# The last batch's channel products as seven block products, with sums of weight blocks kept in DRAM

## The chip, the core and the metric

The kernel runs on one core of one Trainium2 chip. A core has TensorE (matrix products into PSUM; PE in the profile, with PEld for the loading of the stationary operand), VectorE (DVE), ScalarE (ACT), GpSimd (POOL), and SyncE (SP), which here only issues DMA transfers. Each engine works through its own instructions in order and waits for the others on semaphores. The metric is the time of one execution on the device in microseconds.

## The reference

Four batches of 8 heads, 768 positions and 64 elements each go through an attention with a window of 16 positions to each side and 24 block summaries, and the result, x (768 x 512 per batch), through a mixer of two parts:

```python
xt = x.transpose(0, 2, 1)
h = np.maximum(xt @ w_tok1, 0.0) @ w_tok2       # tokens: 768 -> 256 -> 768
u = x + h.transpose(0, 2, 1)
h2 = np.maximum(u @ w_ch1, 0.0) @ w_ch2         # channels: 512 -> 1536 -> 512
return (u + h2).astype(np.float32)
```

The channel products are the largest part: per batch 768 x 512 x 1536, twice. Matrices come in float32 and results are close to float32: every operand of these products is kept as a high part in the TensorE's rounded float32 type and a low part (the rest), and a product is the sum of three: high by high, high by low, low by high.

## The kernel before

All of the program is written as pieces of work with an engine, an estimated duration, the data that they read and write, and a rank. `Plan` (L61 to L185) orders them: a list scheduler runs the engines in estimated time, each engine takes the ready piece with the lowest rank and then the lowest place in the program, and what comes out is the fixed order of every engine's instructions. The ranks are R_H, R_EVAC, R_ATT, R_LATER, R_W (0 to 4).

Buffers are `Slot`s under a tag with a number of buffers. The slots of one tag are taken in the order of the program: a slot's first piece waits until the slot so many places earlier is done with altogether (its stores to DRAM included), and comes no earlier than the first piece of the slot just before it (`_link`, L105 to L115).

Work is staged by batch. The main loop (L1142 to L1208) goes over the batches; for each, 24 slots: half 0 of the positions with 12 chunks of 128 hidden channels, then half 1 with 12. In batches 0 to 2 half 0 has 512 positions and half 1 has 256; in the last batch both have 384. In a slot, `ch1` (L829) makes one chunk of hidden channels, 12 matmuls into a bank with tag mm; ACT and DVE make its relu's high and low part, h. `ch2` (L866) adds that chunk's part to the four output banks acc0 to acc3, 12 matmuls. After the twelfth, `finish` (L917) adds u to the banks, on DVE its high part and on GpSimd its low part, and stores the result. For the half 1 of batches 0 to 2 its one output buffer has tag h.

Between these, the slots of batch b carry the attention of batch b + 1 (`att_step`), then `tok1x` (L703), which makes the first token product for two heads' pairs: three chunks, each with x and w_tok1 split on ACT and GpSimd into buffers xs and ws with tag u0, the products t1q on TensorE. `tok2` (L755) makes the second token product (up), adds x, and splits the sum into u's high and low part. For batches 2 and 3 x comes transposed by way of DRAM (`turn_x`, `fetch_x`). `tok2` for half 0 of batch b + 1 stands in slots 21 and 22 of batch b (23 in batch 0); for half 1 in slots 2 to 5 of batch b + 1 itself (0 for batch 0 and 1). Weights are loaded in batch 0 as 64-bit words, turned into float32 and split (`w_tick`, L997) into w1h, w1l, w2h, w2l, wt2h and wt2l, which stay in SBUF to the end. In the last batch four additions on GpSimd (`residual`, L904) prepare u for its second `finish`.

## Time and profile before

| | before |
|---|---|
| time of three runs | 581.9 us median (580.58 to 582.2) |
| span of the profiled execution | 579.3 us |
| its own time beside the span | the profile states none; the median is 2.6 us over the span |
| TensorE busy | 565.0 us, 98% of the span, 4701 matmuls |
| DVE, ACT, GpSimd busy | 288.2, 216.0, 154.1 us |
| granted TensorE clock | 0.994 of full speed |
| DMA | 75.89 MB, mean 131 GB/s |
| batch 0's first `hp` to batch 1's, 2's and 3's (start) | 65.9, 206.66, 339.53, 472.32 us |

The span is from the first to the last instruction of one execution. A matmul's busy time overlaps with its neighbours', as they are pipelined; how far apart the matmuls of one kind start is read from groups in the chain of waits, where a line has the start, the duration and the count. A group "a<-b" is an instruction that writes tile a and reads tile b. "idle before" is time in which an engine stood still just before such an instruction, with what ended it.

### The profile page before, as it was taken

The numbers are of one execution on the slowest core, as the hardware profiler recorded it, in microseconds if no ns is written. First come the engines' busy times: TensorE is split into PE (matmuls) and PEld (weight loads), VectorE is DVE, ScalarE is ACT, GpSimd is POOL, SyncE is SP. The second block draws the span as 40 slices with busy tenths as digits, with TensorE's granted clock in tenths as the row PEclk, the third lists the DMA queues.
The fourth block names the chain that finished last, engine by engine and source line by source line (L and its number), as shares of the span: only waits on it lengthen the run. The fifth ranks groups of instructions, "written<-read, shape, count | busy, mean of one in ns | idle before, by whom it ended". The sixth has DMA issues, their size and how long they took to land.

```text
span 579.3 us, 12315 instructions
## 1 busy us (share of the span) xinstructions
PE 565.0 (98%) x4701; PEld 500.2 (86%) x4701; DVE 288.2 (50%) x872; ACT 216.0 (37%) x697; POOL 154.1 (27%) x191
## 2 busy tenths in 40 slices
PE   7889999989999999999999999999999999999997
PEld 4678888768999988878899988888799999999997
DVE  3698799997563255644743336452543222112112
ACT  4777565436474343322333224222434111111110
POOL 0236586743033310000085010100085022005000
PEclk9999999989999999999999999999999999999999
DMA  8954568653565027846775127746454012001001
GB/s 281 325 159 129 182 200 262 220 164 129 188 190 161 18 76 197 230 121 188 204 192 131 23 55 189 195 139 139 117 146 81 1 34 59 1 1 54 1 1 54
DMA packets 116778, 75.89 MB, mean 131 GB/s; under 512 B 86640, under 2 KB 100080, under 8 KB 116720
## 3 DMA queue, kind: packets, MB, share of 16 engines
q1 hardware_dynamic: 116432, 74.72, 45.6%
q8 instruction: 37, 0.61, 0.4%
q10 hardware_dynamic: 288, 0.39, 0.2%
q14 instruction: 21, 0.17, 0.1%
HBM read 57.59 MB, written 15.73 MB: 127 GB/s over the span
## 4 chain that ended last, share of the span: by engine, by line
PE 82%; DVE 11%; DMA 3%; issue 2%; ACT 1%; SPq 0%; POOL 0%; DVEq 0%; ACTq 0%
PE acc L882 31%; PE hp L839 30%; PE t1q L736 5%; PE up L779 4%; PE av L559 4%; PE sc L428 4%; DMA w<-in_w_ch 2%; DVE wb L1067 2%; DVE wp L1060 1%; PE et L490 1%; PE warm L1108 1%; DVE wp L1053 1%; DVE wb L1060 1%; DVE vs L384 1%; DVE e L442 1%
## 5 line engine op out<-in xcount | busy, mean ns | idle before, releaser
L882 PE MATMUL acc<-h,w2h 128*128 128x512 f32 (+2 forms) x768 | 207.1, 340 | 2.2 <-DVE h L856 2.2
L839 PE MATMUL hp<-u,w1h 128*128 128x512 f32 (+2 forms) x768 | 192.7, 338 | 0.0
L882 PEld LDWEIGHTS acc<-h,w2h 128*128 128x128 f32 x768 | 135.8, 189 | 17.0 <-DVE h L856 3.4
L839 PEld LDWEIGHTS hp<-u,w1h 128*128 128x128 f32 x768 | 132.6, 189 | 12.3 <-issue 1.3
L856 DVE SCALAR_TENSOR_TENSOR h<-hp,h 128x512 fp32r<-128x512 f32 (+2 forms) x96 | 53.1, 553 | 153.8 <-ACT h L851 153.8
L839 PE MATMUL hp<-u,w1l 128*128 128x512 f32 (+2 forms) x384 | 129.1, 336 | 0.3 <-POOL w1l L1095 0.3
L882 PE MATMUL acc<-h,w2l 128*128 128x512 f32 (+2 forms) x384 | 129.1, 336 | 0.0
L851 ACT ACTIVATE h<-hp 128x512 fp32r<-128x512 f32 (+2 forms) x96 | 46.9, 488 | 201.4 <-PE hp L839 200.4
L452 ACT ACTIVATE e<-e,den 128x120 f32<-128x120 f32 x192 | 73.3, 385 | 48.6 <-DVE den L442 41.1
L839 PEld LDWEIGHTS hp<-u,w1l 128*128 128x128 f32 x384 | 72.5, 189 | 6.6 <-POOL w1l L1095 0.7
L882 PEld LDWEIGHTS acc<-h,w2l 128*128 128x128 f32 x384 | 72.6, 189 | 5.2
L943 POOL TENSOR_TENSOR ot<-ot,u 128x512 f32<-128x512 f32 (+2 forms) x28 | 27.9, 1021 | 116.8 <-DVE ot L935 116.8
L442 DVE CUSTOM_DVE_ANT_0 e<-sc,mask_sb 128x120 f32<-128x120 f32 x192 | 41.4, 277 | 13.7 <-PE sc L428 10.9
L779 PE MATMUL up<-wt2h,t 128*128 128x256 f32 (+2 forms) x128 | 37.6, 351 | 0.5 <-DVE xT L795 0.5
L411 POOL MEMSET e<- 128x48 f32 x16 | 2.2, 138 | 130.1 <-DMA away<-e 69.5
L452 ACT ACTIVATION_READ_ACCUMULATOR e<-e,den 128x1 f32 x192 | 36.3, 189 | 0.0
L722 POOL TENSOR_TENSOR xs<-x,xs 128x512 fp32r<-128x512 f32 x18 | 23.5, 1304 | 27.8 <-ACT xs L717 27.7
L428 PE MATMUL sc<-k,q 64*64 64x120 f32 x768 | 28.6, 275 | 1.9 <-PE et L490 0.7
L428 PEld LDWEIGHTS sc<-k,q 64*64 64x64 f32 x768 | 21.0, 134 | 10.5 <-issue 6.8
L736 PE MATMUL t1q<-xs,ws 128*128 128x256 f32 x216 | 28.9, 284 | 0.0
L559 PEld LDWEIGHTS av<-v,eT 120*64 120x64 f32 x768 | 24.0, 138 | 4.8 <-issue 2.3
L736 PEld LDWEIGHTS t1q<-xs,ws 128*128 128x128 f32 x216 | 27.3, 191 | 0.3
(73 smaller groups left out, 597.0 us busy)
## 6 DMA issues: line engine op xcount, KB each, us to landing
w<-in_w_ch SPq DMA_DIRECT2D x48, 256.0 KB
k<-in_kw SPq DMA_DIRECT2D x16, 720.0 KB
v<-in_vw SPq DMA_DIRECT2D x32, 288.0 KB
q<-in_q SPq DMA_DIRECT2D x16, 384.0 KB
away<-e SPq DMA_DIRECT2D x16, 384.0 KB
eT<-away SPq DMA_DIRECT2D x64, 96.0 KB
w<-in_w_tok SPq DMA_DIRECT2D x12, 256.0 KB
vb<-in_vb SPq DMA_DIRECT2D x32, 96.0 KB
```

The lines of the kernel that those rows point to most:

```text
L428: nc.tensor.matmul(tiles[j].t[c * QT : (c + 1) * QT, i * NC : (i + 1) * NC], lhsT=qt.t[rows, t * QT : (t + 1) * QT], rhs=kt.t[rows, t, :], ...
L442: nc.vector.tensor_tensor_reduce(out=e.t[:, j, i * P : i * P + NC], in0=tiles[j].t[:, i * NC : (i + 1) * NC], in1=mask_sb[:, mv, :], op0=A ...
L452: nc.scalar.activation(ei, ei, AF.Exp, bias=den_t[n].t[:, 1, T : T + 1], scale=-1.0, accum_out=den_t[n].t[:, 0, T : T + 1],)
L559: nc.tensor.matmul(pv[cs, T], lhsT=eT[:NC, T % (TT // 2), cs], rhs=v.t[:NC, 2 * T + c], start=True, stop=True,)
L722: lambda slot=slot, src=src: nc.gpsimd.tensor_tensor(out=slot.t[:, 1], in0=src(), in1=slot.t[:, 0].bitcast(F32), op=ALU.subtract),
L736: nc.tensor.matmul(pt.t[:, 2 * P * k : 2 * P * (k + 1)], lhsT=ws[:, wp, T, ks], rhs=xs[:, xp, T], start=(c == 0 and k == 0 and T == 0 and ...
L779: nc.tensor.matmul(pt.t[:, :nt], lhsT=t1.t[:, part, ks], rhs=w[:, k, h0 : h0 + nt], start=(far and k == 0 and i == 0), stop=(k == DTOK // ...
L839: nc.tensor.matmul(pt.t[:, :nt], lhsT=w[:, c, fs], rhs=us[c].t[:, part], start=(i == 0), stop=(i == len(ops) - 1),)
L851: lambda: nc.scalar.activation(h.t[:, 0], pt.t[:, :nt], AF.Relu),
L856: lambda: nc.vector.scalar_tensor_tensor(out=h.t[:, 1], in0=pt.t[:, :nt], scalar=0.0, in1=h.t[:, 0].bitcast(F32), op0=ALU.max, op1=ALU.sub ...
L882: nc.tensor.matmul(slot.t[:, c0 : c0 + nt], lhsT=w[:, f, o * P : (o + 1) * P], rhs=h.t[:, part], start=(f == 0 and w is w2h and part == 0 ...
L943: lambda view=view, u=u: nc.gpsimd.tensor_tensor(out=view(), in0=view(), in1=u.t[:, 1].bitcast(F32), op=ALU.add),
```

## The change

The two channel products of the last batch are written as 2 x 2 blocks and computed by Strassen's scheme (in Winograd's form) with seven block products in place of eight, in each of the two layers. For the first layer the blocks are: positions 0 to 383 and 384 to 767, input channels in two halves, hidden channels in two halves. For the second: the same positions, hidden channels in two halves, output channels in two halves.

- *Weight sums.* Four sums of weight blocks (s1 to s4) per layer and per pair of hidden chunks, 12 pieces in all. `weight_sums` makes a piece: five operations of 128 x 256 on GpSimd and five on DVE, then high and low part by two copies on ACT and two 128 x 512 subtractions on GpSimd, with a rank of its own, R_BACK, behind all others, and stores both parts to DRAM (2 x 512 KB). Four pieces stand in slots 13, 14, 15 and 17 of each of batches 0 to 2; those of slots 13 and 15 take two buffers each with tag u0, the others two with tag h. `weight_away` stores w2 as it is to DRAM too, in slots 0 to 11 of batch 1.
- *The last batch's input.* `tok2` of both its halves now stands in slots 20 to 22 of batch 2, with all of its x fetched in slots 18 and 19. The full sums stay in SBUF as u32, and of half 1 only the upper channels are split.
- *`last_mix`.* Takes the place of the last batch's 24 slots. It makes the four combinations of u (t1 to t4), on DVE (t1, t2) and GpSimd (t3, and t4's split), with t3's and one of t4's buffers under tag h. Then six steps k over pairs of hidden chunks, each with seven products of 6 matmuls, in the order 11, s2, (s4 and 22 of step k - 1), s3, 12, s1. They accumulate in three banks, which are read out by ACT and DVE between the products. GpSimd makes the combinations of the hidden blocks. The second layer has seven products of six steps, each step with a split on ACT and DVE and 2 x 3 matmuls. The sums s1 to s4 come from DRAM in rings (`first_load`, `second_loads`), in the second layer the single blocks too, into the space of w1 and other buffers. TensorE's order in `last_mix` is chained piece by piece.
- *Tiles.* Weights are per-chunk tiles (`w1_t`, `w2_t`) with high and low part side by side, in buffers that `last_mix` takes over. `residual` goes.

The diff, cut to its core:

```diff
-    w1h = const.tile([P, NC4, DFF], F32R, name="w1h")
...
+    w1_t = [sbuf([P, 2, NC4, P], "w1", f"w1_{f}", NF, F32R) for f in range(NF)]
+    w2_t = [sbuf([P, 2, DM], "w2", f"w2_{f}", NF, F32R) for f in range(NF)]
...
-    R_H, R_EVAC, R_ATT, R_LATER, R_W = range(5)
+    R_H, R_EVAC, R_ATT, R_LATER, R_W, R_BACK = range(6)
...
+    def weight_sums(w, k, tag):
+        blk, keys = blocks(w, k)
+        bufs = BUFS[tag]
+        z = sbuf([P, 4, 256], tag, f"sz_{w}_{k}", bufs)
+        hi = sbuf([P, 4, 256], tag, f"sh_{w}_{k}", bufs, F32R)
+        away = sd[w, k] = plan.slot(dram, [P, 2, 4, 256], F32, "sums", f"sums_{w}_{k}", 2 * HALF)
+        gate = state["gate"]
...
+        step("pool", 0, part("21", 0), part("22", 0), ALU.add)
+        step("pool", 0, own(0), part("21", 1), ALU.add)
+        step("pool", 0, own(0), part("22", 1), ALU.add)
+        step("dve", 2, part("11", 0), part("21", 0), ALU.subtract)
+        step("dve", 2, own(2), part("11", 1), ALU.add)
+        step("dve", 2, own(2), part("21", 1), ALU.subtract)
...
+        step("pool", 1, own(0), part("11", 0), ALU.subtract)
+        step("pool", 1, own(1), part("11", 1), ALU.subtract)
...
+        step("dve", 3, part("12", 0), own(1), ALU.subtract)
+        step("dve", 3, own(3), part("12", 1), ALU.add)
+        for ss in ((0, 1), (2, 3)):
...
+        add(
+            "sp", 0.06, lambda: nc.sync.dma_start(out=away.t[:, 0], in_=hi.t.bitcast(F32)),
...
+    def last_mix():
...
+        tmp = sbuf([P, 4, HS], "wt", "t32", 3)
+        tmp3 = sbuf([P, 2, HS], "h", "t33", 2)
...
+        for j in range(2):
+            both("dve", (tmp, j), (B12, j), (B11, j), ALU.subtract, R_ATT)
+            both("dve", (tmp, 2 + j), (B22, j), (tmp, j), ALU.subtract, R_ATT)
+            split((tmp, 2 + j), *ops["t2"][j], "dve", R_ATT)
+        for j in range(2):
+            both("pool", (tmp3, j), (B22, j), (B12, j), ALU.subtract, R_ATT)
+            split((tmp3, j), *ops["t3"][j], "pool", R_ATT)
...
+        def later(k):
...
+            first(k, "s4", b_, "22", False)
+            from_bank(c12, b_, c12, True)
+            first(k, "22", c_, "t4", False)
+            from_bank(c21, c_, c21, True)
...
+        for k in range(HALF):
...
+            first(k, "11", a_, "11", True)
...
+            first(k, "s2", b_, "t2", True)
+            from_bank(c21, b_, c12)
+            if k:
+                later(k - 1)
+            first(k, "s3", c_, "t3", True)
+            first(k, "12", a_, "21", False)
...
+            first(k, "s1", b_, "t1", False)
+            from_bank(c22, b_, c12)
+            from_bank(c22, c_, c22, True)
...
+        SECOND = (
+            ("11", "h11", "a"), ("s2", "t2", "b"), ("s3", "t3", "c"), ("s1", "t1", "b"),
+            ("12", "h21", "a"), ("s4", "h22", "b"), ("22", "t4", "c"),
+        )
...
-    for b in range(B):
+    for b in range(B - 1):
...
+            t2s = [(20, 0, 0), (20, 0, 1), (21, 1, 0), (21, 1, 1)]
+            t2s += [(22, 1, 2), (22, 1, 3), (22, 0, 2), (22, 0, 3)]
...
+            if b + 1 == B - 1 and slot in (18, 19):
+                for h in range(2):
+                    for p in (2 * slot - 36, 2 * slot - 35):
+                        fetch_x(b + 1, h, p)
...
+            for at_slot, tag in ((13, "u0"), (14, "h"), (15, "u0"), (17, "h")):
+                if slot == at_slot:
+                    n = len(sd)
+                    weight_sums(1 + n // HALF, n % HALF, tag)
+            if b == 1 and slot < NF:
+                weight_away(slot)
             ch2(b, half, f)
-            if last and 14 <= slot < 18:
-                residual(b, 1, slot - 14)
             if f == NF - 1:
                 finish(b, half)
+    last_mix()
     plan.write()
```

More of the change, by code (lines that the diff above doesn't have):

```diff
@@ L39 @@
 HS = S // 2
+HL = ((0, 0), (0, 1), (1, 0))
 HI_MAX = 122879.9921875
@@ L538, in fetch @@
             add(
-                "sp", 0.4, lambda r=r: part(r), reads=[(away, 0)], writes=[(slot, r)], kb=kb,
+                "sp", 0.4, lambda r=r: part(r), reads=[(away, 0)], writes=[(slot, key(r))], kb=kb,
             )
@@ L695, in tok1 @@
         add(
-            "pe", 2.8, products, reads=x_keys(b, p) + [("wt1", i) for i in range(3)],
+            "pe", 2.8, products, reads=x_keys(b, p) + [(wt1, i) for i in range(3)],
             writes=[(pt, 0)], rank=R_ATT,
@@ L790, in tok2 @@
         if far:
-            xT = xT_t.pop((b, half, p))
-            parts = [(xT, r) for r in range(P // 32)]
+            xT, parts = xT_t.pop((b, half, p))
             add(
@@ L845, in ch1 @@
             "pe", 12 * nt / 2220, products,
-            reads=[(u, i) for u in us for i in range(2)] + [("w1", f, 0), ("w1", f, 1)],
+            reads=[(u, i) for u in us for i in range(2)] + [(w1_t[f], 0), (w1_t[f], 1)],
             writes=[(pt, 0)], rank=R_W,
@@ new lines, in finish, with store @@
+            add(
+                "pool", spent(nt, 0.7, 1.2),
+                lambda view=view, u=u: nc.gpsimd.tensor_tensor(
+                    out=view(), in0=view(), in1=u.t[:, 1].bitcast(F32), op=ALU.add
+                ),
+                reads=[(u, 1)], writes=[key], rank=R_ATT,
+            )
+            store(b, h0, nt, o, view, [key])
+    def store(b, h0, nt, o, view, keys, queue="sp"):
+        eng = nc.sync if queue == "sp" else nc.scalar
+        add(
+            queue, 0.06,
+            lambda: eng.dma_start(out=out[b, o * P : (o + 1) * P, h0 : h0 + nt], in_=view()),
+            reads=keys, kb=nt // 2,
+        )
```

483 lines of the change are left out of this document (376 added, 107 removed).

## The prediction

> **What bounds the kernel now.** I read the page's busy shares, slices, transfers and chain of waits first, then TensorE's waits, then the last batch as one stretch. First the page.
>
> ```profile
> span 579.3 us, 12315 instructions
> PE 565.0 (98%) x4701; PEld 500.2 (86%) x4701; DVE 288.2 (50%) x872; ACT 216.0 (37%) x697; POOL 154.1 (27%) x191
> ...
> POOL 0236586743033310000085010100085022005000
> PEclk9999999989999999999999999999999999999999
> ...
> HBM read 57.59 MB, written 15.73 MB: 127 GB/s over the span
> ...
> PE 82%; DVE 11%; DMA 3%; issue 2%; ACT 1%; SPq 0%; POOL 0%; DVEq 0%; ACTq 0%
> ```
>
> TensorE is the bound: 98% busy at full clock, and the chain that ended last is its own work. So a matmul taken away is worth its spacing, as long as nothing that feeds TensorE becomes late. GpSimd is busy 27% on average, but in two bursts (the 85 and 085 of the slices), which matter below.
>
> TensorE's longest wait from 80 to 440 us (total, times, longest), the last batch as a stretch (busy time and count of PE, weight loads, DVE, ACT, GpSimd; clock; DMA share; GB/s), and how fast its matmuls follow each other (chain in order of time, columns start, duration, what):
>
> ```profile
> PE acc L882 <- DVE h L856: 2.2, 2, 1.8
> ```
> ```profile
> 472.30:575.40 103.10, 102.58 (x590) 101.80 (x588) 19.53 (x38) 13.69 (x28) 14.87 (x16) 1.00 0.09 21
> ```
> ```profile
> 478.48 2.08 PE acc L882 x12
> 480.56 0.02 issue
> 480.59 1.31 PE up L779 x6
> 481.89 2.08 PE hp L839 x12
> ```
>
> From the first matmul of the last batch (472.32, row below) to its last (575.24) there are 588 matmuls of 384 columns, 2.08/12 = 0.1736 us each. DVE, ACT and GpSimd are under 20% there, DMA at 9%: that is the cover for what the change adds. The `up` group took 1.31 where six spacings are 1.04: a group that TensorE has to wait for costs about 0.27 more on top of the wait.
>
> **The matmuls.** Before, the last batch's two layers are 2 x 288 = 576 matmuls. After, the first layer has 7 products x 6 steps x 6 matmuls = 252 and the second 7 x 6 x 2 x 3 = 252: 504, of the same shape, each with its own weight load as before. 504 x 0.1736 = 87.5 us. Of `up`, two groups of the last batch (588 - 576 = 12 matmuls, 2.1 us) move ahead of it. So 103.1 - 87.5 - 2.1 = **13.5 us** go; the 0.5 us of waiting and the slow `up` starts in the old stretch are in that.
>
> The tail stays: one DVE addition after the last matmul, one store of 192 KB, as in these rows. From 575.58 to the span's end are 3.7 us before and after.
>
> ```profile
> 575.24 0.34 PE L882 MATMUL acc<-h,w2h 128*128 128x384 f32 x1
> ```
>
> **The third product of the first step (s3 x t3).** t3 is made on GpSimd in a buffer with tag h. Buffers of a tag are taken in the order of the program, and that one comes behind the output buffer of batch 2's second half (`finish`), so the first of its instructions is put in order only when the first addition of that `finish` starts. From then GpSimd has, by rank and sequence, four `finish` additions ahead of most of t3. The rows are GpSimd's and DVE's timeline at that place, and the groups of its 384-wide work:
>
> ```profile
> 471.82 1.46 DVE L935 TENSOR_TENSOR ot<-acc,u 128x256 f32<-128x256 f32 x4 [1.28 <-PE acc L882]
> ```
> ```profile
> 472.32 2.81 POOL L943 TENSOR_TENSOR ot<-ot,u 128x256 f32<-128x256 f32 x4 [28.38 <-DVE ot L935]
> ```
> ```profile
> L856 DVE SCALAR_TENSOR_TENSOR h<-hp,h 128x384 fp32r<-128x384 f32 x24 | 13.3, 556 | 68.7 <-ACT h L851 68.7
> L851 ACT ACTIVATE h<-hp 128x384 fp32r<-128x384 f32 x24 | 11.8, 491 | 78.4 <-PE hp L839 78.4
> ...
> L808 POOL TENSOR_TENSOR u<-xT,u 128x384 fp32r<-128x384 f32 x4 | 4.1, 1015 | 9.7 <-ACT u L802 9.7
> ...
> L802 ACT ACTIVATE u<-xT 128x384 fp32r<-128x384 f32 x4 | 2.1, 524 | 9.8 <-DVE xT L795 9.8
> ```
> ```profile
> 472.32 0.52 PE L839 MATMUL hp<-u,w1h 128*128 128x384 f32 x2
> ```
>
> The additions start with the new batch (call it 0) and end at 2.81. Then the split of t3's first half (1.02, to 3.83), the subtraction for its second (to 4.84), ACT's copy (0.52 and two handovers of about 0.1, to 5.56), its split (to 6.58). TensorE has done 11 and s2 at 2.08; it takes the first four matmuls of s3 from 3.8 and the last two at 6.6, and ends s3 at 7.0 where 3 x 1.04 = 3.1 is due: **+3.9 us**. Queued behind it are 12, s1 and all later products (an order chained by hand). Ends: 0, if t3's instructions go ahead of the additions, and 6.8, if the weight sums of slot 17 still hold the output buffer (6.2 us of GpSimd by the prices below, half of it late). I take 3.9, the row's case. Three waits restart TensorE: 3 x 0.27 = **+0.8** (0 to 3).
>
> **The weight sums.** Twelve pieces, four in each of batches 0 to 2, at slots 13, 14, 15 and 17. Each has on GpSimd five 256-wide and two 512-wide operations, on DVE five 256-wide, on ACT two copies, on SP two stores of 512 KB. Prices:
>
> ```profile
> L1095 POOL TENSOR_TENSOR w2l<-wb,w2h x24: 737/748/1194, 58.5 to 133.3; 128x256 fp32r<-128x256 f32 x24
> ```
> ```profile
> L722 POOL TENSOR_TENSOR ws<-wt,ws x18: 1277/1290/1312, 163.4 to 442.6; 128x512 fp32r<-128x512 f32 x18
> ```
> ```profile
> 290.00:340.00 50.00, 50.00 (x427) 48.49 (x426) 18.77 (x37) 14.88 (x31) 21.09 (x20) 1.00 0.44 99
> 421.00:472.00 51.00, 51.00 (x439) 50.48 (x438) 15.35 (x32) 14.10 (x31) 20.23 (x16) 1.00 0.26 62
> ```
>
> GpSimd per piece: 5 x 0.75 + 2 x 1.29 = 6.3 us; four are 25 us. In the second halves of batches 1 and 2 it has 50 - 21.1 = 28.9 and 51 - 20.2 = 30.8 us free: they fit, barely. But slots 13 and 15 use tag u0, whose four buffers come ahead of those of `tok1x`: its first chunk now waits until slot 13's sums are in DRAM, its second until slot 15's are. In batch 1 the second half's `finish` additions are over at 294.7 (four of 1.28 from 289.6). Three pieces end at about 294.7 + 19 + 2.6 (the first chunk between) = 316 to 317; with 3.5 for the store (a load of half the size took 2.9) 320.5. Five more chunks at 2 x 1.29, and their matmuls, end at 336; before, `tok1x` was done by about 320, and 14 us of the two layers' matmuls lay behind:
>
> ```profile
> 289.59 2.55 POOL L943 TENSOR_TENSOR ot<-ot,u 128x512 f32<-128x512 f32 x2 [9.54 <-DVE ot L935]
> ```
> ```profile
> 84.72 2.90 DMA w<-in_w_ch
> ```
> ```profile
> 180.43 3.06 PE t1q L736 x24
> ```
> ```profile
> 318.18 1.44 PE t1q L736 x12
> ...
> 322.48 2.80 PE up L779 x12
> ...
> 339.53 2.76 PE hp L839 x12
> ```
>
> The last two `up` groups (1.40 each) then end near 340 and their splits at 342; batch 2's first product needs its fourth block 9/12 of 2.76 us after 339.5, at 341.6. So some 0.4 late by this count; I take **+1.5**, as GpSimd's queue is full for 45 us and anything late stays late (0 to 7, below). In batch 2 the additions can be over at 426: 426 + 19 + 2.6 + 3.5 + 15.4 = 467 for the last of `tok1x`; t1's split 1.2, two `up` groups 2.1 and t2 (three DVE operations, a copy) 2.5 make 472.6 to 472.9, and s2 needs it at 472.3 + 2.1 + 1.0 = 475.4: **0** (to 3.8). In batch 0 `tok1x` ran mostly from 180 on, 40 us after its slot 13: 0. If the cover by the two layers' matmuls were gone, all of the 25 us per batch would show.
>
> DVE and ACT get 20 x 0.37 (the row of four in 1.46) and 8 x 0.6 us per batch, beside matmuls. What can harm is that GpSimd's price isn't fixed: the same operations of both engines, apart and at the same time:
>
> ```profile
> 107.12 1.44 POOL L1095 TENSOR_TENSOR w1l<-wb,w1h 128x256 fp32r<-128x256 f32 x2
> ...
> 112.72 2.32 POOL L1095 TENSOR_TENSOR w1l<-wb,w1h 128x256 fp32r<-128x256 f32 x2
> ```
> ```profile
> L1067 DVE SCALAR_TENSOR_TENSOR wb<-w,wb 128x512 int32<-128x512 int32 x9 | 8.0, 885 | 0.3
> ...
> L1067 DVE SCALAR_TENSOR_TENSOR wb<-w,wp 128x512 int32<-128x512 int32 x10 | 6.9, 686 | 0.3
> ```
>
> The same pair on GpSimd took 1.44 or 2.32, so 0.44 more for each operation; on DVE 885 ns with both inputs in SBUF against 686 with one in PSUM. The Trainium skill (SBUF — State Buffer, section Who interferes with whom) says that a DVE instruction with two SBUF inputs and a GpSimd one that reads SBUF exclude each other for a whole instruction. The trace agrees, 1194 against 748 ns for one. By that rule the sums would cost the second rival's time, without it the forecast's.
>
> **DMA and the last batch's other engines.** New: 24 sums stores and 12 copies of w2 (18.9 MB) in batches 0 to 2, 66 loads of 256 KB (17.3 MB) in the last 95 us, 182 GB/s where 21 ran. The nearest row:
>
> ```profile
> 60.00:130.00 70.00, 67.44 (x324) 54.30 (x324) 65.49 (x120) 36.73 (x89) 46.22 (x65) 0.98 0.66 208
> ```
> ```profile
> L951 SPq DMA_DIRECT2D out<-ot x28: 332/376/1172, 141.8 to 534.0; - x28
> ```
> ```profile
> L532 SPq DMA_DIRECT2D xT<-xaway x64: 557/622/1198, 308.8 to 484.1; - x64
> ```
> ```profile
> 433.73 0.98 DVE L634 STREAM_TRANSPOSE xb<-x 128x768 f32<-128x768 f32 x1
> ```
>
> 208 GB/s at two thirds of the engines: it fits, with up to 12 ring buffers of lead. SP issues them in 66 x 0.38 us. Moved: the 16 fetches of the last batch's second half (0.62 each, 10 us of SP) go from its own slots 2 to 5 to slots 18 and 19 of batch 2, past that half's `finish` stores; they need `turn_x`'s stores only, whose transpose ends at 434.7, and are due at 468 and later. DVE has in the last batch about 84 operations of 0.56 (47 us of 88), ACT 74 of 0.5, GpSimd some 35 of 1.0: beside TensorE. Each first-layer bank is read out (about 1.2 us) while two or more other products run (2.1 us). 0 us (to +5).
>
> **Sum.** -13.5 + 3.9 + 0.8 + 1.5 = -7.3; the span 579.3 becomes 572.0. The runs' median, 581.9, is 2.6 over this span (launch and end, which the trace doesn't show), so **574.6 us**.
>
> **Rivals.** (1) *The cover holds*: t3 comes in time and the sums hide. 581.9 - 13.5 = 568.4. For it: TensorE's longest wait there was 1.8 us; against: the buffer order, which is in the code. (2) *GpSimd's queue ahead of* `tok1x`: the 20 DVE operations of each batch's four pieces each stop a GpSimd one for 0.44, 8.8 us in a queue that is full. Lateness L costs 0.4 + L in batch 1 and L - 2.8 in batch 2; with the 4.7 above the gain is gone from L = 5.6, and slower shows from 6.5. At 8.8: 572.0 - 1.5 + 9.2 + 6.0 = 585.7, or 588; with 15 collisions 584. I put it at 586. It is the other side. Against: GpSimd's median of 748 ns says that most don't meet. (3) *Weights late*: the second layer eats 1.57 MB per 6.2 us, 250 GB/s, more than 208; once the 12 buffers of lead are used up, some 5 us: 580. (4) *It doesn't gain what it says*: each of 84 steps with an operand fresh from DVE restarts TensorE at 0.27, 22 us: 596. Against: `hp` and `acc` follow each other at 2.08 without a gap.
>
> **How the numbers follow.** Forecast 0.51 (its own range 570.5 to 579), rivals 0.23, 0.14, 0.07, 0.05. The range reaches over (1) and up to 583.5, short of (2)'s upper part and (4). A measurement tells about 0.3% (1.7 us) from no change. Faster: 0.47 of the forecast, (1), half of (3): 0.73. Same: 0.11. Slower: (4) and most of (2), 0.16.
>
> **What would show it.** 4629 matmuls; the last 504 in 88 us plus waits; a wait of TensorE on GpSimd of about 4 us in the last batch's third product; GpSimd's tenths near 9 in the second halves of batches 1 and 2, `tok1x`'s matmuls some 15 us later there, and a wait of 1 to 2 us before batch 2's first `hp`; HBM writes of 15.7 + 18.9 MB. Wrong it is if TensorE waits elsewhere by more than 3 us, above all in the second layer, or if t3's split comes ahead of the four additions.

## The result and the profile after

The changed kernel takes 602.99 us (median, 601.85 to 605.36), the kernel before 582.05 beside it: a ratio of 1.0357, 95% interval 1.0319 to 1.0396. It is slower, where 574.6 was forecast and the range ended at 583.5. The page of the profiled execution after:

```profile
span 602.3 us, 12729 instructions
...
PE 568.4 (94%) x4629; PEld 495.3 (82%) x4629; DVE 383.0 (64%) x994; ACT 257.2 (43%) x777; POOL 265.5 (44%) x301
...
POOL 0226586736872700000387850010059895344611
PEclk9889999999999999999999899999999998999999
...
HBM read 74.90 MB, written 34.60 MB: 182 GB/s over the span
```

The counts came as foreseen (4629 matmuls, 34.6 MB written), but TensorE's share fell from 98% to 94%: 602.3 - 568.4 = 33.9 us of the span have no matmul in them, where 14.3 had none before. Where they lie shows in a table of stages, in us, taken from the profiled executions. A stage of a batch runs from the first `hp` of a half to the next; the last batch runs from its first matmul to the end of its last.

| stage | before | after | the change with stores only (below) |
|---|---|---|---|
| batch 0, second half | 70.2 | 78.2 | 69.8 |
| batch 1, first half | 79.9 | 78.4 | 78.4 |
| batch 1, second half | 53.0 | 66.2 | 65.7 |
| batch 2, first half | 79.2 | 81.6 | 82.0 |
| batch 2, second half | 55.8 | 66.0 | 55.2 |
| last batch | 101.2 | 91.9 | 97.8 |

Before, the last batch's 2.1 us of `up` that the change moves are counted with batch 2 already (53.7 + 2.1, 103.3 - 2.1). The last batch gained 9.3 us, the second halves lost 8.0 + 13.2 + 10.2 = 31.4, and the two first halves of the table came out 0.9 longer together (-1.5 and +2.4). The second halves are the stretches in which attention for the next batch and `tok1x` run, and in which the sums stood. Their rows (the columns are as in the prediction's stretches: PE, weight loads, DVE, ACT, GpSimd; clock; DMA share; GB/s), first after, in the order of batches 1, 0, 2, then before:

```profile
292.90:359.20 66.30, 60.36 (x518) 56.01 (x518) 41.44 (x89) 23.57 (x63) 50.32 (x51) 0.95 0.70 192
136.40:214.60 78.20, 72.36 (x793) 67.15 (x792) 55.36 (x163) 39.47 (x130) 50.17 (x51) 0.98 0.53 175
440.70:506.70 66.00, 59.11 (x470) 56.24 (x468) 42.39 (x67) 21.82 (x49) 54.71 (x52) 0.97 0.55 157
```
```profile
286.40:339.40 53.00, 53.00 (x446) 51.20 (x445) 21.55 (x43) 15.71 (x35) 20.89 (x20) 1.00 0.47 113
136.30:206.50 70.20, 70.20 (x794) 66.12 (x792) 36.86 (x140) 35.27 (x120) 20.91 (x20) 1.00 0.42 130
418.60:472.30 53.70, 53.70 (x457) 52.99 (x456) 17.57 (x38) 14.97 (x36) 20.23 (x16) 1.00 0.28 65
```

Before, TensorE was busy in every microsecond of the three. After, it lacks 5.8 to 6.9 in each, and part of what it has runs at a lower granted clock (0.95 to 0.98). In batch 1 it also has 72 matmuls more (518 against 446): they ran in the first half before, which is shorter for it. GpSimd has 29 to 34 us more per batch, where 25 were priced; DVE has 18.5 to 24.8 more, where 20 x 0.37 = 7.4 were. TensorE's longest waits there, first in batch 0, then in batch 1, then in batch 2 (total, times, longest):

```profile
PE et L488 <- DVE x L569: 3.9, 3, 1.4
```
```profile
PE t1q L746 <- POOL ws L732: 1.9, 2, 1.3
```
```profile
PE up L790 <- DVE t L685: 1.9, 1, 1.9
```

So in the main it is late work of DVE that TensorE waits for in batches 0 and 2, and of GpSimd in batch 1. The groups of the sums on both engines (shortest, median, longest ns):

```profile
L984 POOL TENSOR_TENSOR sz<-sz,w x48: 724/797/924, 146.5 to 477.2; 128x256 f32<-128x256 f32 x48
L984 DVE TENSOR_TENSOR sz<-sz,w x36: 382/852/1529, 145.9 to 478.5; 128x256 f32<-128x256 f32 x36
```

Of the 60 additions and subtractions of 128 x 256 on DVE, 52 ran while GpSimd had an operation with two inputs under way: their median is 0.85 us, the longest 1.53. The other 8 have a median of 0.41. On GpSimd the same kind took 0.80 beside DVE's sums and 0.74 without them. The last batch itself, from its first matmul to half a microsecond before the end of its last:

```profile
506.70:598.10 91.40, 89.39 (x503) 87.85 (x503) 56.17 (x89) 39.51 (x80) 38.57 (x35) 1.00 0.57 184
```

The chain of waits gives its second layer's first four products as 6.36 us each for 36 matmuls, without an idle time between them; two of the rows:

```profile
553.90 6.36 PE qa L1095 x36
560.26 6.36 PE qb L1095 x36
```

6.36/36 = 0.1767 us, nearly the 0.1736 of the old layers: weights in time, no restart per step. The first layer took 47.1 us where 252 x 0.1736 = 43.7 were due. TensorE's longest wait in it is 1.4 us, for t2 on DVE; for t3, which the prediction had waiting for GpSimd, it doesn't wait at all here.

### The profile page after: what moved, and what is told of

It reads as the page before. It is cut to its first block, busy times and chain, and to the rows that moved or that the text cites. A ratio compares the mean times of both kernels' runs of the same rounds, so it can differ in the third digit from the quotient of the medians.

```text
span 602.3 us, 12729 instructions
## 1 busy us (share of the span) xinstructions
PE 568.4 (94%) x4629; PEld 495.3 (82%) x4629; DVE 383.0 (64%) x994; ACT 257.2 (43%) x777; POOL 265.5 (44%) x301
## 5 line engine op out<-in xcount | busy, mean ns | idle before, releaser
L896 PE MATMUL acc<-h,w 128*128 128x512 f32 (+1 forms) x864 | 167.0, 342 | 4.5 <-DVE h L870 4.4
L853 PE MATMUL hp<-u,w 128*128 128x512 f32 (+1 forms) x864 | 165.5, 341 | 0.8 <-ACT u L817 0.6
L896 PEld LDWEIGHTS acc<-h,w 128*128 128x128 f32 x864 | 134.1, 189 | 25.8 <-DVE h L870 5.6
L853 PEld LDWEIGHTS hp<-u,w 128*128 128x128 f32 x864 | 134.2, 190 | 21.8 <-issue 1.3
L865 ACT ACTIVATE h<-hp 128x512 fp32r<-128x512 f32 (+1 forms) x72 | 35.1, 487 | 130.6 <-PE hp L853 130.4
L870 DVE SCALAR_TENSOR_TENSOR h<-hp,h 128x512 fp32r<-128x512 f32 (+1 forms) x72 | 39.6, 549 | 66.0 <-ACT h L865 66.0
L790 PE MATMUL up<-wt,t 128*128 128x512 f32 (+2 forms) x192 | 42.3, 360 | 4.3 <-DVE t L685 2.7
L1460 POOL TENSOR_TENSOR w<-wb,w 128x256 fp32r<-128x256 f32 x48 | 38.0, 810 | 18.1 <-ACT w L1454 17.7
L984 POOL TENSOR_TENSOR sz<-sz,w 128x256 f32<-128x256 f32 x48 | 37.9, 790 | 3.3
L1015 POOL TENSOR_TENSOR sz<-sz,sh 128x512 fp32r<-128x512 f32 x24 | 32.8, 1373 | 9.5 <-ACT sh L1010 4.7
L426 PEld LDWEIGHTS sc<-k,q 64*64 64x64 f32 x768 | 21.1, 135 | 10.8 <-issue 6.6
```

What stands on the lines that cost most here:

```text
L426: nc.tensor.matmul(tiles[j].t[c * QT : (c + 1) * QT, i * NC : (i + 1) * NC], lhsT=qt.t[rows, t * QT : (t + 1) * QT], rhs=kt.t[rows, t, :], ...
L790: nc.tensor.matmul(pt.t[:, :nt], lhsT=t1.t[:, part, ks], rhs=wt2[w].t[:, k, h0 : h0 + nt], start=(far and k == 0 and i == 0), stop=(k == D ...
L853: nc.tensor.matmul(pt.t[:, :nt], lhsT=w1_t[f].t[:, w, c], rhs=us[c].t[:, part], start=(i == 0), stop=(i == len(ops) - 1),)
L865: lambda: nc.scalar.activation(h.t[:, 0], pt.t[:, :nt], AF.Relu),
L870: lambda: nc.vector.scalar_tensor_tensor(out=h.t[:, 1], in0=pt.t[:, :nt], scalar=0.0, in1=h.t[:, 0].bitcast(F32), op0=ALU.max, op1=ALU.sub ...
L896: nc.tensor.matmul(slot.t[:, c0 : c0 + nt], lhsT=w2_t[f].t[:, w, o * P : (o + 1) * P], rhs=h.t[:, part], start=(f == 0 and w == 0 and part ...
```

## Experiments: what the sums' arithmetic costs

Four kernels were measured together (before there: 581.58 us). The first leaves the sums' arithmetic out and keeps buffers and stores:

```diff
-        step("pool", 0, part("21", 0), part("22", 0), ALU.add)
...
-                "pool", 1.1,
...
+            lambda: nc.scalar.activation(
+                hi.t.rearrange("p a c -> p (a c)"),
...
+            reads=keys, writes=[(hi, ss) for ss in ((0, 1), (2, 3))], rank=R_BACK, behind=gate,
...
```

> Left out: the arithmetic of the weight sums; two ScalarE copies of weight tiles fill the same buffers, and the same stores follow, so the last batch computes with other numbers. Theory A (GpSimd's queue ahead of the token product makes the second halves of batches 0 to 2 longer: 8, 13 and 11 us): the 25 us of GpSimd per batch go, the buffer order stays with copies and stores only; 573 to 578 us, second halves within 3 us of before's 70.2, 53.0 and 53.7 (+2.1). Theory B (the 19 MB of extra stores delay other transfers): little changes, 598 to 605. Theory C (VectorE's sums hold up the hidden layer's splits, whatever GpSimd does): as A, 572 to 578; this run doesn't tell A from C.

594.03 us, 1.0213 [1.0172, 1.0254]. The second leaves out the buffers and the ACT copies too and stores the weight tiles as they are:

```diff
-        z = sbuf([P, 4, 256], tag, f"sz_{w}_{k}", bufs)
-        hi = sbuf([P, 4, 256], tag, f"sh_{w}_{k}", bufs, F32R)
...
+        for i in range(2):
+            t = (w1_t, w2_t)[w - 1][k + HALF * i]
...
+                reads=[(t, 0), (t, 1)], writes=[(away, i)], kb=524, behind=gate,
```

> Left out: the arithmetic of the weight sums and their buffers; weight tiles are stored as they are, same bytes to DRAM, so the last batch computes with other numbers. Theory A: 571 to 574 us; what it is below the run with copies is the price of the buffer order by itself (0 to 5 us). Theory B: 598 to 605. In both, the last batch keeps about 91 us, and if t3's wait for GpSimd was only hidden by the late start, the third product now waits some 4 us.

590.9 us, 1.0159 [1.0138, 1.0179]. Both fall between the two theories. Without the arithmetic the whole is 603.0 - 594.0 = 9.0 us shorter, without buffers and copies 3.1 more, and with neither of them 590.9 is still 9 us slower than before and 16 above the forecast. So the sums' arithmetic is a cause, and not the only one; which of its two engines costs the time these two runs don't tell. By stages (the table's last column) the sums cost 8.4, 0.5 and 10.8 us in the three second halves; that the whole differs by less is the last batch, which now takes 97.8 us in place of 91.9, as the third product waits.

The third does all sums on VectorE, in the change's places and buffers:

```diff
-        step("pool", 0, part("21", 0), part("22", 0), ALU.add)
+        step("dve", 0, part("21", 0), part("22", 0), ALU.add)
...
-                "pool", 1.1,
-                lambda cs=cs: nc.gpsimd.tensor_tensor(
+                "dve", 0.62,
+                lambda cs=cs: nc.vector.tensor_tensor(
```

> The sums stay where the change put them, but all of their additions and subtractions are on VectorE; GpSimd has none of them. Theory A: the chain ahead of the token product stays through the buffers, but GpSimd's 25 us go and VectorE's five and a half per piece replace them: 583 to 593 us. Theory C: VectorE has twice the work (22 us more per batch) in front of the hidden layer's splits: 600 to 615.

595.29 us, 1.0234 [1.0212, 1.0257]: between the two theories again, and 7.7 us faster than the change, though one engine now has all ten steps. Its group of the sums:

```profile
L984 DVE TENSOR_TENSOR sz<-sz,w x84: 382/424/1399, 143.3 to 466.7; 128x256 f32<-128x256 f32 x84
```

More than twice as many instructions, the median back at 0.42: only 9 of all 120 now meet a two-input operation of GpSimd, and those 9 have a median of 1.17. So what lengthened them to 0.85 was GpSimd at work beside them. The Trainium skill (SBUF — State Buffer, section Who interferes with whom) says that which of the two blocks is decided by the order of issue. The trace agrees: in the change 45 of the 52 that met a GpSimd operation began after it, and DVE paid; in the rows of the prediction it was GpSimd. How much of the 7.7 us is these collisions and how much GpSimd's shorter queue, this run doesn't tell, as it takes away both.

The fourth moves the pieces to the first halves, in four 2 KB buffers of tag t1:

```diff
-            for at_slot, tag in ((13, "u0"), (14, "h"), (15, "u0"), (17, "h")):
+            for at_slot, tag in [(n, "t1") for n in ((8,10,12,14) if b == 0 else (6,8,10,12))]:
...
+        zs = [sbuf([P, 2, 256], tag, f"sz_{w}_{k}_{i}", bufs) for i in range(2)]
```

> All the work of the change, with the weight sums moved: slots 8, 10, 12, 14 of batch 0 and 6, 8, 10, 12 of batches 1 and 2, in the four 2 KB buffers of tag t1 (stores of 256 KB), not in those of the token product. Theory A: GpSimd is nearly idle there (0.3 us of 20), so the second halves return to 70, 53 and 54+2 us: 572 to 577 us, faster than both kernels. Theory C: VectorE's 20 operations per batch still meet GpSimd's and hold up the hidden layer's splits: 582 to 592. Theory B: 598 or more.

600.11 us, 1.0335 [1.0288, 1.0382], in the range of theory B. The stages tell more than the whole: batch 2's halves were 81.8 and 55.7 us, as with no arithmetic at all (82.0 and 55.2); batch 1's second half stayed at 65.8; batch 0's was 76.6. So in batch 2 the first half hides the sums, and batch 1 has another trouble.

## Experiments: the stores

All of this section and the next leave the sums' arithmetic out as the second kernel above does, so that 590.9 us is what they are held against (before here: 580.95 us). First, no stores but one pair, from which all rings are read:

```diff
-        for i in range(2):
+        for i in range(2 if (w, k) == (1, 0) else 0):
...
-            if b == 1 and slot < NF:
-                weight_away(slot)
```

> No sums and no copies of w2 are stored but one pair (1 MB) in batch 0, from which the last batch reads every block of its rings, so the reads of the last batch and its 504 products stay and the output isn't the reference's. If the stores are the whole of batch 1's loss, its second half is 53-55 us and the kernel takes 577-581. If something else in the changed weight tiles or in the order causes it (rival), the second half stays above 60 us and the whole at 586-591. The first layer's wait for t3 stays in both: some 9 us over 252 x 0.1736 = 43.7 us.

578.18 us, 0.9943 [0.9916, 0.997]; batch 1's second half 52.5 us. The stores cost 590.9 - 578.2 = 12.7 us, all of it where the prediction said 0. Then the two kinds of stores apart. The copies of w2 moved to batch 0:

```diff
-            if b == 1 and slot < NF:
-                weight_away(slot)
+            if b == 0 and 12 <= slot < 24:
+                weight_away(slot - 12)
```

> The kernel with the stores only (590.9 us; no arithmetic of sums, weight tiles stored as they are, so the output isn't the reference's), with one move: the twelve 512 KB stores of the second layer's weights go from batch 1's slots 0 to 11 to batch 0's slots 12 to 23. Its batch 1 loses 12.7 us in the second half against the kernel before (65.7 against 53.0). Theory D (these stores keep the DMA engines behind through batch 1, so that attention's turned tiles land late): batch 1's second half falls to 54-57 us and the whole to 579-583, unless batch 0's second half pays (then it grows by what batch 1 gains, and the whole stays at 588-591). Rival S (the sums' own stores, issued among attention's in the second half, are what counts): batch 1's second half stays at 63-66 and the whole at 588-592.

593.65 us, 1.0226 [1.02, 1.0252], a little above the ranges of both theories. Batch 1's second half is 52.5 us, but batch 0's 85.2 instead of 69.8: what batch 1 gains, batch 0 pays, and more. The sums' stores of batch 1 moved to its last slots:

```diff
-            for at_slot, tag in ((13, "u0"), (14, "h"), (15, "u0"), (17, "h")):
+            for at_slot in ((20, 21, 22, 23) if b == 1 else (13, 14, 15, 17)):
```

> The kernel with the stores only (590.9 us), with another move: batch 1's four pairs of sums' stores go from slots 13, 14, 15, 17 to slots 20 to 23, where the DMA engines of the kernel before stand idle (0.00 in 325-339 us). Theory S (those stores stand ahead of attention's transfers): batch 1's second half falls to 54-57 us and the whole to 579-583. Theory D (the w2 copies of the first half are the cause): it stays at 62-66 us, the whole at 587-592. If both are needed to fill the DMA engines, each move alone gains most of the loss.

584.24 us, 1.0048 [1.0026, 1.0071]; batch 1's second half 55.2 us, batch 2's first 85.9 instead of 82.0. So each move alone frees the stretch: it was the sum of both on top of attention's traffic. How that reaches TensorE, in the kernel with stores only: SP's timeline (start, duration, what), then stretches of 6 us.

```profile
302.01 1.44 SPq L979 DMA_DIRECT2D sums<-w  x2
303.50 7.07 SPq L530 DMA_DIRECT2D eT<-away  x4
...
311.30 0.98 SPq L979 DMA_DIRECT2D sums<-w  x2
```
```profile
303.00:309.00 6.00, 6.00 (x53) 6.00 (x52) 1.56 (x4) 1.43 (x4) 1.37 (x2) 1.00 1.02 349
...
321.00:327.00 6.00, 6.00 (x54) 6.00 (x53) 0.85 (x2) 0.77 (x2) 0.00 (x0) 1.00 0.00 1
...
333.00:339.00 6.00, 3.38 (x24) 2.98 (x24) 0.42 (x1) 1.15 (x2) 4.12 (x4) 1.00 0.88 222
339.00:345.00 6.00, 1.38 (x6) 1.38 (x7) 2.36 (x4) 0.63 (x1) 1.56 (x2) 0.63 0.69 146
```

Attention's turned tiles (`eT`) are fetched from DRAM behind the sums' stores in one queue, at a DMA share of 1.02. Attention was late already when the half began, as 96 products with these tiles are left for it in place of 48 (rows below). The last products with them (`av`) start at 306.4 us in the kernel before and here at 329.2, 45.1 us into the half instead of 20.0 (first the kernel before):

```profile
L559 PE MATMUL av<-v,eT x48: 222/222/270, 305.0 to 306.4; 120*64 120x64 f32 x48
```
```profile
L557 PE MATMUL av<-v,eT x96: 222/222/270, 291.2 to 329.2; 120*64 120x64 f32 x96
```

Until 327 the two layers' matmuls cover this; `tok1x` and `up`, which need x, then run with nothing behind them: 1.38 of 6 us busy, clock 0.63. The DMA engines meanwhile did nothing from 321 to 327.

## Experiment: the third product

The last batch's operands are prepared ahead of batch 2's last `finish` in the order, so that t3 takes its buffer first, and s3 goes to the end of its step:

```diff
             if f == NF - 1:
+                if (b, half) == (B - 2, 1):
+                    mix = last_mix()
+                    next(mix)
                 finish(b, half)
-    last_mix()
+    next(mix, None)
...
-            first(k, "s3", c_, "t3", True)
             first(k, "12", a_, "21", False)
...
             from_bank(c22, b_, c12)
+            first(k, "s3", c_, "t3", True)
             from_bank(c22, c_, c22, True)
```

> The kernel with the stores only (590.9 us), with the last batch's operands (t2, t3, t1, t4) prepared ahead of batch 2's last finish in the order, so that t33 takes its buffer before finish's output does, and the product 12 and s1 of each first-layer step ahead of s3. Theory W (the wait for t3 and the lower granted clock that follows it cost the first layer's 9 us): the first layer falls from 52.9 us to 44-46, the granted clock stays 1.00 there, the whole is 582-585. Rival (the clock falls in the first layer whatever its operands do, or the wait turns up at another operand): first layer 49-53 us, the whole 587-592.

584.43 us, 1.0068 [1.0045, 1.0091]; the first layer falls from 52.9 to 46.0 us. What was there without the edit, in the kernel with stores only: GpSimd's, ACT's and TensorE's timeline (in brackets the idle time before, and what ended it), then the stretches behind it.

```profile
487.00 2.81 POOL L935 TENSOR_TENSOR ot<-ot,u 128x256 f32<-128x256 f32 x4 [9.07 <-DVE ot L927]
489.77 0.99 POOL L1026 TENSOR_TENSOR t<-t,t 128x384 fp32r<-128x384 f32 x1
490.72 1.00 POOL L1011 TENSOR_TENSOR t<-u,u 128x384 f32<-128x384 f32 x1
492.77 1.97 POOL L1026 TENSOR_TENSOR t<-t,t 128x384 fp32r<-128x384 f32 x2 [1.05 <-ACT t L1020]
```
```profile
492.17 0.94 ACT L1020 ACTIVATE t<-t 128x384 fp32r<-128x384 f32 x2 [3.39 <-DVE t L1011]
```
```profile
487.01 1.23 PE L1053 MATMUL pa<-u,w 128*128 128x384 f32 x6
...
490.82 0.61 PE L1053 MATMUL pc<-t,s 128*128 128x384 f32 x2 [1.33 <-POOL t L1026]
493.16 0.45 PE L1053 MATMUL pc<-t,s 128*128 128x384 f32 x1 [1.73 <-ACT t L1020]
494.79 1.01 PE L1053 MATMUL pc<-t,s 128*128 128x384 f32 x2 [1.19 <-POOL t L1026]
495.60 2.12 PE L1053 MATMUL pa<-u,w 128*128 128x384 f32 x6
497.52 2.12 PE L1053 MATMUL pb<-t,s 128*128 128x384 f32 x6
499.44 1.91 PE L1053 MATMUL pa<-u,w 128*128 128x384 f32 x6
501.19 1.03 PE L1053 MATMUL pb<-t,s 128*128 128x384 f32 x5
```
```profile
492.00:496.00 4.00, 1.66 (x5) 1.40 (x6) 0.69 (x2) 0.94 (x2) 1.97 (x2) 0.77 0.88 288
496.00:500.00 4.00, 4.00 (x14) 4.00 (x13) 0.32 (x1) 1.01 (x2) 1.01 (x1) 0.50 0.21 70
```

The order on GpSimd is the one that the prediction read from the buffers, four additions first. The product after s3 starts at 495.60 where 490.1 was due: 5.5 us. Two copies on ACT start only at 492.17, after a DVE subtraction that belongs to t4, though GpSimd had t3's second half ready at 491.72: t4's copy stands first in ACT's order, and its split first in GpSimd's. And then the granted clock goes to 0.50, and the next products start 1.92, 1.92 and 1.75 us apart instead of 1.04, another 2.5 us. With t3 early the same stretch has its clock:

```profile
488.50:492.50 4.00, 4.00 (x25) 4.00 (x24) 1.10 (x3) 0.98 (x2) 1.91 (x3) 1.00 0.49 146
```

## Experiments: all together

First the three moves with stores only: sums' stores at slots 13, 15, 17, 19, 21 / 18, 20, 22 / 13, 15, 17, 19 of the three batches, copies of w2 six each in batches 1 and 2, and the edit of the last section.

```diff
-            if b == 1 and slot < NF:
-                weight_away(slot)
+            if b in (1, 2) and slot < HALF:
+                weight_away(slot + HALF * (b - 1))
...
+            for at_slot, tag in [(n, "h") for n in ((13, 15, 17, 19, 21), (18, 20, 22), (13, 15, 17, 19))[b]]:
```

> Stores only (no arithmetic of sums, weight tiles stored as they are, so the output isn't the reference's), with the three moves together: sums' stores at slots 13, 15, 17, 19, 21 of batch 0, 18, 20, 22 of batch 1 and 13, 15, 17, 19 of batch 2; the copies of w2 six in batch 1 and six in batch 2 (slots 0 to 5); the last batch's operands ahead of batch 2's finish and s3 last in its step. If the losses found so far are separate (10.5 us in batch 1's second half, 6.9 in the first layer), 590.9 - 10.5 - 6.9 = 573.5: 571 to 577. If one only hides another, 580 or more.

574.15 us, 0.9868 [0.9852, 0.9885] (before there: 582.01). The losses were separate and add up. The last batch takes 90.2 us here, 11.0 less than before. With the arithmetic put back in those places, in tag h's two buffers alone, on VectorE:

```diff
-        step("pool", 0, part("21", 0), part("22", 0), ALU.add)
+        step("dve", 0, part("21", 0), part("22", 0), ALU.add)
...
```

> The whole computation: as the kernel with the stores spread, and the sums' arithmetic all on VectorE, in the two buffers of tag h (none in tok1x's), so that one piece follows another. Theory (the arithmetic costs only where it holds tok1x's buffers or makes VectorE and GpSimd collide): 574 to 580 us. Rival (56 us of VectorE work in second halves delay attention's own VectorE work wherever they stand, as the 3.6 and 5 us of batches 0 and 2 with all sums on VectorE): 581 to 590.

627.4 us, 1.0772 [1.0746, 1.0797]. With the change's division between the engines, that is with `weight_sums` as the change has it and only its places and tag other:

```diff
-            for at_slot, tag in ((13, "u0"), (14, "h"), (15, "u0"), (17, "h")):
+            for at_slot, tag in [(n, "h") for n in ((13, 15, 17, 19, 21), (18, 20, 22), (13, 15, 17, 19))[b]]:
```

> As the kernel before this one in the list, but with the sums' arithmetic on GpSimd and VectorE as the change has it (five instructions and both low parts of a piece on GpSimd). If the two engines' collisions cost (a VectorE addition of 128x256 took 0.91 us in the changed kernel, 0.41 alone), this is 4 to 10 us above the kernel with all on VectorE: 580 to 590. If they lie beside idle time once tok1x's buffers are free, it is within 2 us of it.

630.69 us, 1.0833 [1.0814, 1.0851]. And on VectorE with six pieces in each of batches 0 and 2, none in batch 1:

```diff
+            for at_slot, tag in [(n, "h") for n in ((12, 14, 16, 18, 20, 22), (), (12, 14, 16, 18, 20, 22))[b]]:
```

> The whole computation on VectorE again, six pieces in batch 0 and six in batch 2 (slots 12, 14, 16, 18, 20, 22), none in batch 1, whose DMA engines were the busiest. If batch 1 is the only place where a piece costs, 573 to 578 us; if a piece costs about 1 us wherever it stands (3.6 us for four in batch 0, 5 in batch 2 with all sums on VectorE), 580 to 586.

632.07 us, 1.0868 [1.0842, 1.0894]. All three expectations missed by some 50 us. A piece needs both buffers of tag h until its stores have landed, so five in a row reach into the next first half, where `h` itself has that tag. Two of TensorE's waits in the first of the three kernels, one in batch 1's first half, one in the last batch's first layer (total, times, longest), and what GpSimd waited for there before it began t3 (in brackets):

```profile
PE acc L896 <- ACT h L865: 8.6, 1, 8.6
```
```profile
PE pc L1095 <- ACT t L1062: 9.0, 1, 9.0
```
```profile
524.66 1.95 POOL L1053 TENSOR_TENSOR t<-u,u 128x384 f32<-128x384 f32 x2 [30.06 <-DMA sums<-sh]
```

The first is a single wait of 8.6 us for an h; the second is for t3, whose buffer has that tag too and comes free with a store of the sums. In the third kernel, with six in a row in batches 0 and 2, the same two waits are 16.2 and 18.0 us, and batch 2's first half, with no piece ahead of it, takes 80.8. These runs tell nothing of the arithmetic itself. For that, most pieces went to the first halves of batches 1 and 2, in tag t1's buffers, where GpSimd had 3.7 of 79.9 us to do before, and the copies of w2 to the last slots:

```diff
+            for at_slot, tag in (
+                [(14, 'u0'), (15, 'h'), (17, 'u0')],
+                [(6, 't1'), (8, 't1'), (10, 't1'), (12, 't1')],
+                [(6, 't1'), (8, 't1'), (10, 't1'), (12, 't1'), (15, 'h')],
+            )[b]:
...
+            wf = {(1, 19): 0, (1, 20): 1, (1, 21): 2, (1, 22): 3, (2, 16): 4,
...
```

> The whole computation. Sums: three pieces in batch 0's second half on VectorE (tags u0, h, u0), four in each of the first halves of batches 1 and 2 in four 2 KB buffers of tag t1 with the change's division between GpSimd and VectorE, one in batch 2's second half (h, VectorE); copies of w2 in the last slots of batches 1 and 2, where the DMA engines were idle; the last batch's operands early and s3 last in its step. Theory P (the arithmetic costs through its place and buffers; the first halves of batches 1 and 2 took 78.4 and 81.8 us with it, as without): 574.2 + 3 x 0.9 for batch 0's pieces = 577, 575 to 580. Rival E (the arithmetic costs about 1 us a piece wherever it stands): 584 to 590.

584.41 us, 1.0042 [1.002, 1.0065]: the rival's number, for a reason that shows two kernels further on. With all of its arithmetic on VectorE:

```diff
-        step("pool", 1, own(0), part("11", 0), ALU.subtract)
+        step("dve", 1, own(0), part("11", 0), ALU.subtract)
...
-                "pool", 1.1,
-                lambda z=z, hi=hi: nc.gpsimd.tensor_tensor(
+                "dve", 0.62,
+                lambda z=z, hi=hi: nc.vector.tensor_tensor(
```

> The kernel with the pieces in the first halves, all arithmetic on VectorE. Theory P: within 2 us of the division between the two engines. Rival X (what a piece costs are collisions of VectorE and GpSimd, 0.91 us for a VectorE addition in place of 0.41): 3 to 6 us below it.

588.11 us, 1.0106 [1.0067, 1.0145]: 3.7 us above, so no collision that it avoids is worth VectorE's added time. There were few to avoid: with the division, 21 of 80 VectorE additions met a GpSimd operation, where 52 of 60 do in the change. And with the one piece of batch 2's second half moved to batch 0:

```diff
-                [(14, 'u0'), (15, 'h'), (17, 'u0')],
+                [(13, 'u0'), (14, 'h'), (15, 'u0'), (17, 'h')],
...
-                [(6, 't1'), (8, 't1'), (10, 't1'), (12, 't1'), (15, 'h')],
+                [(6, 't1'), (8, 't1'), (10, 't1'), (12, 't1')],
```

> The kernel with the pieces in the first halves, with four in batch 0's second half (slots 13, 14, 15, 17) and none in batch 2's second half. With all sums on VectorE four pieces there had cost 3.6 us (73.4 against 69.8): so batch 0's second half some 1 us above the one with three pieces, and the whole within 1.5 us of it.

578.0 us, 0.9927 [0.9901, 0.9953] (before: 581.83): faster than both kernels, and 5 us better than expected. The first halves of batches 1 and 2 were 81.2 and 80.1 us in it and 80.0 and 80.9 with stores only: eight pieces at about nothing, so "it costs a microsecond wherever it stands" falls. Not that second halves as such charge: the last of the four pieces ran over into the second half each time (in batch 2 as 5 of its operations on VectorE and 5 on GpSimd), and these halves took 53.8 and 56.8 us, with stores only 53.6 and 56.7. But batch 2's single piece more cost 62.5 - 56.8 = 5.7 us, and batch 0's four 74.4 - 69.6 = 4.8. Batch 2's second half with that piece and without, and in the former TensorE's longest wait:

```profile
424.70:487.20 62.50, 58.00 (x472) 56.30 (x469) 45.33 (x81) 24.04 (x58) 36.37 (x29) 0.97 0.66 195
```
```profile
425.50:482.30 56.80, 55.70 (x472) 54.57 (x469) 35.21 (x69) 22.79 (x56) 35.27 (x29) 1.00 0.68 197
```
```profile
PE acc L896 <- ACT h L865: 2.7, 1, 2.7
```

One piece brought DVE 10 us of work. For 3.5 us of them its low parts (L1015, 1.74 each, 0.68 alone) ran while GpSimd made those of the piece that had run over (from 447.32 to 450.49). Behind them on DVE stood attention's x; for that x ACT waited 3.75 us with a split of `tok1x`, and behind this split in ACT's order stood the h that the two layers were waiting for. DVE's row and ACT's:

```profile
447.55 3.48 DVE L1015 TENSOR_TENSOR sz<-sz,sh 128x512 fp32r<-128x512 f32 x2
```
```profile
452.06 0.63 ACT L727 ACTIVATE xs<-x 128x512 fp32r<-128x512 f32 x1 [3.75 <-DVE x L569]
```

Behind that wait, from 454.7 to 460.7 us, the granted clock was 0.73. The price isn't fixed by the place either: with all sums on VectorE in the change's places, four pieces cost 60.4 - 55.2 = 5.2 us in this half.

Three last kernels ask what it is in batch 0. In the first, its pieces stand at slots 16 to 19:

```diff
-                [(13, 'u0'), (14, 'h'), (15, 'u0'), (17, 'h')],
+                [(16, 'u0'), (17, 'h'), (18, 'u0'), (19, 'h')],
```

> The kernel with four pieces in batch 0 (578.0 us; its second half there 74.4 us, 69.6 with stores only), these at slots 16 to 19 in place of 13, 14, 15, 17, in the same buffers u0, h, u0, h. Theory V (VectorE was full with attention's work in 146 to 176 us): batch 0's second half 70-72 us, the whole 574-576. Rival T (the buffers of tag u0 hold tok1x back, more so the later a piece stands): 74-78 us there, the whole 578-582.

582.38 us, 1.0008 [0.9975, 1.004]; the half took 79.2 us. In the second, they use h and t1 in turn, none of `tok1x`'s input buffers:

```diff
+                [(16, 'h'), (17, 't1'), (18, 'h'), (19, 't1')],
```

> As the kernel before it in the list, with tags h and t1 in place of u0 and h (the two pieces in t1 divided between GpSimd and VectorE as the change has it). Theory V: within 1 us of the other. Rival T: 70-72 us in batch 0's second half, 3 us or more below the other.

583.68 us, 1.0036 [1.0009, 1.0063]; 81.4 us, so without `tok1x`'s buffers it is no faster. In the third, they are back at 13, 14, 15, 17 and only the planned durations on VectorE are longer:

```diff
-                eng, 0.8 if eng == "pool" else 0.34,
+                eng, 0.8 if eng == "pool" else 0.55,
...
-                "dve", 0.62,
+                "dve", 0.9,
```

> The kernel with four pieces in batch 0 (578.0 us; batch 0's second half 74.4 us), the sums' planned durations on VectorE raised from 0.34 to 0.55 us and from 0.62 to 0.9. Theory O (the order, made with too short durations, is at fault): batch 0's second half 71 to 73 us, the whole 575 to 577. Rival V (VectorE is full there, however it is ordered): 74 to 76 us there, the whole 577 to 580.

578.51 us, 0.9957 [0.9938, 0.9976]; 76.6 us, so better estimates don't help. Neither "VectorE is full" nor "the buffers" wins alone. From 146 to 166 us, before and in the kernel of 578.0 us:

```profile
146.00:156.00 10.00, 10.00 (x137) 9.29 (x133) 4.92 (x23) 4.85 (x18) 0.00 (x0) 1.00 0.82 264
156.00:166.00 10.00, 10.00 (x153) 9.35 (x154) 7.12 (x44) 7.26 (x28) 3.85 (x4) 1.00 0.47 116
```
```profile
146.00:156.00 10.00, 8.78 (x96) 7.65 (x91) 9.75 (x37) 5.22 (x20) 0.00 (x0) 1.00 0.88 255
156.00:166.00 10.00, 10.00 (x170) 8.90 (x169) 9.87 (x42) 6.47 (x26) 0.00 (x0) 1.00 0.60 202
```

VectorE is at 9.75 and 9.87 of 10. With longer estimates TensorE stays busy there, and the loss comes back 30 us later, in `tok1x`:

```profile
186.00:196.00 10.00, 7.18 (x51) 6.58 (x51) 7.26 (x16) 3.62 (x7) 4.75 (x5) 0.93 0.51 197
```

Whether another arrangement of batch 0 would save its 4.8 us stays open; without them the kernel would be near the 574 of the stores alone.

## Why the prediction was wrong

A ledger by the stages of the profiled executions: the last batch -9.3, where -13.5 + 3.9 + 0.8 = -8.8 were forecast; the second halves +31.4, where +1.5 was. Of the 31.4, batch 1's stores are 65.7 - 53.0 = 12.7, and the sums' arithmetic, copies and buffers 8.4 + 0.5 + 10.8 = 19.7; apart from these the second halves of batches 0 and 2 were 1.0 us shorter. The first halves add 0.9. Together +23.0: the span went from 579.3 to 602.3.

- **The matmuls, -13.5: right.** 504 at 0.1736 to 0.1767 us. The second layer ran without waits, so rivals 3 (weights late) and 4 (a restart at each step) fall.
- **"208 GB/s at two thirds of the engines: it fits ... 0 us (to +5)": the step that failed first, 12.7 us.** The step compared averages. It looked at the 182 GB/s of the last batch, which were harmless, and not at batch 1's second half, where transfers that attention waits for take 1.02 of the engines in the first 5.6 us already before:

```profile
286.40:292.00 5.60, 5.60 (x38) 5.11 (x37) 4.71 (x11) 1.46 (x5) 2.41 (x2) 1.00 1.02 267
```

  That row was there to be read. That SP's stores stand ahead of `eT` in one queue was not considered, though it was for `fetch_x`.
- **The weight sums, "+1.5 ... in batch 0: 0 ... in batch 2: 0": mis-sized, 19.7 us in the second halves, and with the wrong bearer.** GpSimd's queue ahead of `tok1x` was seen rightly, and the waits for `xs`, `ws` and t1 in batch 1 are there. But its share of batch 1 is small (66.2 us with arithmetic, 65.7 without, 65.8 with it in the first half): the stores alone make that half as long. The cost shows in batch 0 (78.2 against 69.8) and batch 2 (66.0 against 55.2), both put at 0. "DVE ... get 20 x 0.37 ... beside matmuls" was the other fault: 0.85 us in the middle, and attention's and the two layers' own operations queued behind, as the waits of batches 0 and 2 show. What share the collisions have and what share GpSimd's queue stays open. The second rival has these collisions, but lets GpSimd lose 0.44 each. Its 584 to 588 came nearer; its mechanism is a part of the 19.7 us. A smaller slip in the same step: it has the `finish` additions of batch 1 over at 294.7, but in the kernel before two of the four came behind a chunk of `tok1x` and ended at 297.2.
- **s3's wait, +3.9 and restarts +0.8: not in the change.** There TensorE doesn't wait for t3. As batch 2 ends with the late `up`, GpSimd's `finish` additions are done before t3 is begun; the first layer's 3.3 us too much (47.1 against 43.7) have waits of 1.4 us for t2 and 0.7 for a hidden block in them. That the sum of the last batch came out so near is luck. In the kernel with stores only, where batch 2 is in time, the path is the one that was read from the buffers, and its size was not: 5.5 us of wait, as t4's copy and split stand ahead of t3's, and then 2.5 us of lower clock, which the prediction didn't have.

The forecast's number was met in the end, by a kernel without arithmetic and with every store moved (574.15). That is a coincidence too: there the last batch gains 11.0 us, without a wait for t3, and other stages lose 3.4. The gain of the scheme is real, and what the change pays is for where its by-work stands. The whole computation came to 578.0 at best.

## What to carry to other kernels

An average DMA share says nothing of a stretch in which something waits for transfers: look at the stretch, and at what stands ahead of the urgent transfer in its queue. Work for idle engines belongs where the profile shows them idle and no buffer of the main path is held: eight pieces of sums begun in first halves cost about nothing, and one more, begun in a second half on an engine that others were waiting for, cost 5.7 us. Saved matmuls show at once in their own stage; compare stage by stage, as a gain of 9.3 us and losses of 31 us are one number in the time.

## What was not expected of the hardware

- A stretch with little work is enough for the clock to fall. In the kernel with stores only TensorE never waited longer than 1.73 us around s3, but from 490.8 to 494.2 us it had 1.06 us of work (three matmuls, in the rows above). The granted clock was 0.65 from 494.0 to 494.5 and 0.50 from there to 500.0. The Trainium skill (TensorE: Matmul & The Clock Gate, Part 1: The HAM clock gate) names an idle window of about 3.4 us; here a nearly idle one did.
- When VectorE and GpSimd work on two-input operations at the same time, the loss can fall on VectorE almost alone: 0.85 against 0.42 us there, 0.80 against 0.74 on GpSimd (its median with the pieces in first halves, where most didn't meet):

```profile
L1043 POOL TENSOR_TENSOR sz<-sz,w x32: 722/737/1020, 238.3 to 443.4; 128x256 f32<-128x256 f32 x32
```
